# Beside the FFN: a unit's product on GpSimd, its split into planes on ScalarE, and one product of the ninth tile behind a unit

## Chip, cores and metric

The kernel runs on one core of one Trainium2 chip, as a single launch. The metric is the time of an execution on the device in microseconds. The profile names the engines PE (TensorE matmuls), PEld (TensorE weight loads), DVE (VectorE), ACT (ScalarE), POOL (GpSimd) and SP (SyncE, which here only issues DMAs).

## What is computed

Four sequences of 12544 positions and 128 channels go through a Hyena filter, a causal convolution as long as the sequence, and the result through a maxout FFN with three input matrices:

```
u = x * v                                        # (4, 12544, 128)
h = (relu(pos_emb @ w1) @ w2) * exp(-0.01*pos)   # (12544, 128)
y = irfft(rfft(u, 2S) * rfft(h, 2S))[:S]         # along the sequence
a = (x * y).reshape(4*12544, 128)
out = max(a @ W1, a @ W2, a @ W3) @ w_out        # d_ff = 768
```

## The kernel before

All arithmetic is in fp32. The Fourier transforms are products with constant matrices, in two stages: a first one over 98 blocks, a second one over the 128 positions of a block. The FFN's three-way maximum is rewritten: W1 is subtracted from W2 and W3, so a step makes `max(relu(a @ (W2-W1)), a @ (W3-W1))`, and W1's part is folded with `w_out` into one 128 x 128 matrix `lin` that is applied at the end of a tile.

**Order of the work.** The order is written out by hand; every engine runs its instructions in the order in which the program issues them. A prologue makes the filter's transform and the whole convolution of the first batch (to about 310 us). Then the FFN of batch b runs beside the convolution of batch b+1, for b = 0, 1, 2; the FFN of the last batch ends the kernel. A batch has 32 tiles of 4 x 98 = 392 columns, and a tile has six slots (one for each 128 rows of d_ff), so slot s = 6 i + f is step f of tile i. In a slot the loop calls `up` (two pairs of TensorE products into two of the three PSUM banks `hps`, a relu on ScalarE at L738, a maximum on VectorE at L741 that makes `hid`), then what is due of the down products, and then whatever the dictionaries `stream` and `beside` hold for this slot.

The first eight tiles (`TP = 8`) are taken in pairs with a Strassen-like scheme: their down products (L802) need sums of `hid` tiles that GpSimd makes (`sum_`, L771), and lie in `stream` several slots later, with banks `ops` and `cps3`; results leave through `copied` on ScalarE (L816) and `added` on VectorE (L819). From the ninth tile (i = 8) on, each tile is done by itself: `down` runs two slots late from the list `late`. At f = 0 it starts with the product of `lin` (L156, `ops<-gt,lin`) into the bank `ops`, which the last pair has used.

**Units.** `conv_steps` fills `beside`. The convolution's input for a batch is cut into 32 units of four channels each; in the first stage six units of batch 1 are made in the prologue, so 26, 32 and 32 units are made beside the three FFNs. A unit that is joined at slot s passes through:

- `u_load` (L354), slot s-9: SP issues the DMAs of `xr` and `vr` into two `ut` tiles of 128 x 392
- `u_mul` (L361), slot s-6: the product x * v in place, an elementwise product of two SBUF tiles
- `u_planes` (L381, L382), slot s-5: a memset of the padding and a copy that splits the fp32 numbers into two planes of uint16 halves, into one of three `planes` buffers (tag `cb`)
- `u_dma` (L388), slot s-4: SP issues a transposing DMA of the planes
- `u_join` (L397), slot s: two copies put the transposed halves together again, one on ScalarE and one on VectorE
- `unit` (L413 to L425), slot s+1: `u_first` twice, each 8 TensorE products (16 records in the trace) with the constant `f1q` into a bank `cps`, a copy `high` on ScalarE (L423), a sum and a difference `spec` on VectorE (L425)

The units follow each other every 1.5 to 1.6 slots and take the first 50 to 60 slots of a batch. After them come the pairs of frequencies (`g_quarter` and so on) in the remaining slots. In the same slots GpSimd also makes the sums and differences `t_sums` (L703) of the tile that comes two later, from the tiles `zt` that SP loads; `t_last` makes the tile's inverse transform and `gt`.

Of the kernel before, what the change touches and what calls it, by code (L numbers as in the profile page):

```python
# [13 lines left out]
ALU = mybir.AluOpType  # L14
# [77 lines left out]
def kernel(  # L92
# [15 lines left out]
    nc = tc.nc  # L108
# [247 lines left out]
            ts.append(t)  # L356
        us[u] = ts

    def u_mul(u):
        a, v = us[u]  # L360
        nc.vector.tensor_tensor(out=a[:], in0=a[:], in1=v[:], op=ALU.mult)  # L361

    def turn(u, ps):
        a, _ = us.pop(u)
# [13 lines left out]
    def u_planes(u):  # L378
        a, _ = us.pop(u)
        pl_ = cvp.tile([P, 2, 4, P], U16, tag="cb", name="planes", bufs=3)  # L380
        nc.gpsimd.memset(pl_[:, :, :, NB:], 0)  # L381
        nc.gpsimd.tensor_copy(  # L382
            pl_[:, :, :, 0:NB], a[:].bitcast(U16).rearrange("p s (n h) -> p h s n", h=2))
        us[u] = pl_

# [41 lines left out]
    def unit(u):  # L427
        for h in range(2):
            u_first(u, 2 * h, 2)
# [152 lines left out]
    def conv_steps(b, done):  # L582


        out = []

        def at(slot, late, fn, *args):
            out.append((slot, late, len(out), fn, args))

        for u in range(4, done):
            at(2 * u - 7, 1, unit, u)
        per_pair = 170 / (NK + LATE + 0.6 * (NU - done))
        for u in range(done, NU):
            s = (u - done) * 0.6 * per_pair + 9
            at(max(0, int(s) - 9), 0, u_load, b, u)
            at(int(s) - 6, 0, u_mul, u)
            at(int(s) - 5, 0, u_planes, u)
            at(int(s) - 4, 0, u_dma, u)  # L600
            at(int(s), 0, u_join, u)
            at(int(s + 1), 1, unit, u)
        s0 = int((NU - done - 1) * 0.6 * per_pair + 9) + 6

        def start(x):
            return s0 + int(x // 2 * 2 * per_pair)

        load = [0.6] * (NT * NF)
        for x in range(NK + LATE):
            s = start(x)  # L610
            load[s] -= 1.2
            load[s + 1 + x % 2] += 1.4

        def emptiest(among, cost):
            s = min(among, key=lambda i: load[i])
            load[s] += cost
            return s

        plan = []
        folds = {start(x) + 1 for x in range(NK + LATE)}  # L620
        for i in range(NT - 1):
            s = i * NF
            last = min((3, 4, 2), key=lambda k: s + k in folds)
            load[s + last] += 0.6
            if s <= s0:
                plan.append((0, 0, last))
                continue
            a = emptiest(range(s, s + 2), 0.7) - s
            plan.append((a, emptiest(range(s + a, s + max(a + 1, last - 1)), 0.7) - s, last))
        plan.append((3, 3, 4))  # L630

        for x in range(NK + LATE):
            s, odd = start(x), x % 2
            g, z = x if x < NK else None, x - LATE if x >= LATE else None
            at(s, 1, g_quarter, g, z)
            at(s + 1 + odd, 0, g_fold, g, z)
            at(max(s - 4, LOADS), 0, w_load, x)
            if z is not None:
                at(s + 3 + odd, 0, g_store, b, z)
            if g is None:  # L640
                continue
            if g % 2 == 0:
                at(max(s - 4, LOADS), 0, q_load, g, min(2, NK - g))
                at(s - 1, 0, h_load, g, min(2, NK - g))
            first = s + 2 + 2 * odd
            at(first, 0, q_swap, g, 0)
            at(first + 1, 0, q_swap, g, 64)
            last = start(x + LATE) - 1
            a = emptiest(range(first + 1, min(first + 3, last - 1) + 1), 0.7)
            at(a, 0, q_re, g)  # L650
            a = emptiest(range(a, min(first + 4, last - 1) + 1), 0.7)
            at(a, 0, q_im, g)
            two = sorted(emptiest(range(a + 1, last + 1), 0.55) for _ in range(2))
            for q in range(2):
                at(two[q], 0, q_unfold, g, q)
        slots = {}
        for s, _, _, fn, args in sorted(out, key=lambda r: r[:3]):
            slots.setdefault(s, []).append((fn, args))
        return slots, plan, s0
# [4 lines left out]
    TP = 8  # L664
# [187 lines left out]
    def run(steps):  # L852
        for fn, args in steps:
            fn(*args)
# [22 lines left out]
    def up_pair(b, i, h, j, tag=None):  # L877
        name, f = ORDER[j]
        own = ("hid", 3) if tag or name in sp["hid"] else (name, BUFS[name])
        h[name, f] = up((b, i + int(name[1]) - 1), f + (NC if name[2] == "2" else 0), *own)  # L880
# [46 lines left out]
    for i in range(9):  # L927
        if i < 8:
            mlp_in(i)
        if i:  # L930
            mlp_out(i - 1)
        if i in (4, 5):
            u_mul(i - 4)
        if i == 7:
            turn2(0)
# [3 lines left out]
    for f in range(0, FO, 4):  # L939
        quad([hs[:, f + i] for i in range(4)], (f1h[:, 0], f1h[:, 1]), specH[:, :, :, f:f + 4])  # L940
        u, k = divmod(f // 4, 4)
# [11 lines left out]
    for u in range(0, NU, 2):  # L953
        t = uts.pop(u)
        for v in range(2):
            if u + 4 < NU:
                u_mul(u + 4 + v)
            at = 4 * (u + v)
# [11 lines left out]
    for i in (1, 2):  # L970
        nc.vector.tensor_tensor(out=w_sb[i][:], in0=w_sb[i][:], in1=w_sb[0][:],
                                op=ALU.subtract)
# [173 lines left out]
    for n, (b, i) in enumerate(tiles[:LAST]):  # L1146
        if i == 0:
            beside, plan, pairs_from = conv_steps(b + 1, EARLY if b == 0 else 0)
            turns_.close()
            sp["pool"] = turns_.enter_context(tc.tile_pool(name="stp", bufs=1))  # L1150
            turn_of["of"] = 3
        if n == 0:
            t_load(*tiles[0])
            t_load(*tiles[1])
            t_sums(tiles[0], nc.vector)
            unit(2)
            t_last(tiles[0])
            unit(3)
            t_sums(tiles[1], nc.vector)
        for f in range(NF):  # L1160
            s = i * NF + f
            turn_ = i == NT - 1
            if i < TP:
                i0, j = i - i % 2, i % 2 * NF + f
                if j == 0:
                    h = {}
                    ends = i0 + 2 == TP
                if j in (0, 6 if ends else 4):
                    t_load(b, i0 + 2 + (j > 0))
                up_pair(b, i0, h, j)  # L1170
                if late:
                    down(*late.pop(0))
                if n == 0 and f == 0:
                    t_last(tiles[1])
                elif weights:
                    out, a1, a2 = weights.pop(0)
                    nc.vector.tensor_tensor(out=out, in0=a1, in1=a2, op=ALU.subtract)
                if j == 0:
                    banks = (obank, singles[3])
                    down_pair(b, i0, h, banks if i0 % 4 == 0 else banks[::-1], s, ends,  # L1180
                              1 if ends else 2)
            else:
                if i < NT - 2:
                    if f == 0:
                        t_load(*tiles[n + 2])
                elif turn_ and f < 2:
                    t_load(*tiles[n + 1 + f])
                if turn_ and f == 4:
                    t_sums(tiles[n + 2], nc.vector)
                h_ = up((b, i), f)  # L1190
            if i < TP and not ends:
                if j in (3, 7):
                    t_sums((b, i0 + 2 + (j > 3)))
            elif i >= TP - 1:
                for a in range(2):
                    if f == plan[i][a]:
                        t_sums(tiles[n + 1],
                               nc.vector if turn_ or i * NF > pairs_from else nc.gpsimd, (a,))
            run(stream.pop(s, ()))
            if i >= TP:  # L1200
                late.append(((b, i), f, h_))
                if len(late) > 2:
                    down(*late.pop(0))
            if i < TP and not ends:
                if j in (7, 10):
                    t_last((b, i0 + 2 + (j > 7)))
            elif i >= TP - 1:
                if f == plan[i][2]:
                    t_last(tiles[n + 1])
                if turn_ and f == 5:  # L1210
                    t_last(tiles[n + 2])
            if i >= TP and turn_of["of"] == 3 and not stream:
                turns_.close()
                wp = turns_.enter_context(tc.tile_pool(name="wp", bufs=3))
                hh = turns_.enter_context(tc.tile_pool(name="hh", bufs=2))
                turn_of["of"] = 4
            run(beside.pop(s, ()))
            if s == NT * NF - 1:
                assert not beside and not stream, sorted(beside)
# [72 lines left out]
```

## Time and profile before

| | us |
|---|---|
| median of 3 runs | 2301.78 |
| lowest, highest | 2295.15, 2305.05 |
| the profiled execution, its own time | 2307.12 |
| span of its profile | 2305.3 |

| group of the profile | count | busy us | mean ns |
|---|---|---|---|
| L361 on DVE, product of a unit (all 128 units) | 128 | 90.5 | 707 |
| L382 on POOL, copy into planes | 90 | 79.6 | 885 |
| L381 on POOL, memset of the padding | 90 | 26.6 | 295 |
| L397 on DVE, join | 90 | 87.7 | 975 |
| L397 on ACT, join | 90 | 70.1 | 779 |
| L771 on POOL, `s<-hid`, sums of the pairs | 84 | 94.7 | 1128 |
| L738 on ACT, relu | 768 | 382.5 | 498 |
| L741 on DVE, maximum | 768 | 427.8 | 557 |

Units are made beside the FFN from about 316 to 440 us, 834 to 984 us and 1357 to 1515 us of the span. A row of the timeline gives the start, the time taken, engine, line and operation, out<-in, the count of merged instructions, and in brackets how long the engine was idle before it and what ended that wait. "Busy" of PE is modelled, since matmuls overlap.

### The profile page before, as it was taken

The numbers are of one execution on the slowest core, as the hardware profiler recorded it, in microseconds if no ns is written. First come the engines' busy times: TensorE is split into PE (matmuls) and PEld (weight loads), VectorE is DVE, ScalarE is ACT, GpSimd is POOL, SyncE is SP. The second block draws the span as 40 slices with busy tenths as digits, with TensorE's granted clock in tenths as the row PEclk, the third lists the DMA queues.
The fourth block names the chain that finished last, engine by engine and source line by source line (L and its number), as shares of the span: only waits on it lengthen the run. The fifth ranks groups of instructions, "written<-read, shape, count | busy, mean of one in ns | idle before, by whom it ended". The sixth has DMA issues, their size and how long they took to land.

```text
span 2305.3 us, 70310 instructions
## 1 busy us (share of the span) xinstructions
PE 2260.9 (98%) x28383; PEld 1424.8 (62%) x28383; DVE 1605.3 (70%) x3102; ACT 1203.6 (52%) x2218; POOL 1015.8 (44%) x1207
## 2 busy tenths in 40 slices
PE   8999989999999999999999999999999999999998
PEld 7989857755555557755555557755555556666665
DVE  5588968757878768758887858757887854445443
ACT  2688845456666535546666635546666632222222
POOL 2044447613333347713333347723333326666666
PEclk9999989999999999999999999999999999999999
DMA  8779969789999669969999759969999832222221
GB/s 193 174 222 273 303 160 185 142 197 248 231 232 240 178 141 195 179 147 240 245 251 243 200 131 187 175 144 232 252 248 249 224 91 57 55 58 69 65 55 22
DMA packets 485568, 411.16 MB, mean 178 GB/s; under 512 B 341305, under 2 KB 387866, under 8 KB 485242
## 3 DMA queue, kind: packets, MB, share of 16 engines
q1 hardware_dynamic: 459778, 334.30, 64.9%
q0 software_dynamic: 24752, 70.65, 10.4%
q8 instruction: 223, 3.65, 0.7%
q10 hardware_dynamic: 712, 1.70, 0.3%
q14 instruction: 103, 0.84, 0.1%
HBM read 262.84 MB, written 84.67 MB: 151 GB/s over the span
## 4 chain that ended last, share of the span: by engine, by line
PE 78%; DMA 12%; DVE 3%; SPq 2%; POOL 2%; issue 1%; ACT 1%; POOLq 0%; DVEq 0%; ACTq 0%
PE hps L156 35%; PE ops L156 10%; PE ops L802 7%; PE cps L413 4%; DMA ht<-hd 4%; PE ps L156 3%; DMA wt<-wq_const 3%; PE cps L156 3%; PE ps L165 3%; DMA zt<-zd 2%; PE cps L472 2%; PE sps L1038 2%; PE cps L482 2%; PE cps L802 2%; PE gps L1020 2%; PE last L156 1%
## 5 line engine op out<-in xcount | busy, mean ns | idle before, releaser
L156 PE MATMUL hps<-gt,w_sb 128*64 128x392 f32 x6144 | 1149.2, 495 | 3.4 <-DVE hid L741 2.7
L738 ACT ACTIVATE hid<-hps 128x392 f32<-128x392 f32 x768 | 382.5, 498 | 720.5 <-PE hps L156 667.5
L156 PEld LDWEIGHTS hps<-gt,w_sb 128*64 128x64 f32 x6144 | 431.2, 137 | 418.5 <-issue 369.6
L741 DVE TENSOR_TENSOR hid<-hid,hps 128x392 f32<-128x392 f32 x768 | 427.8, 557 | 352.0 <-PE hps L156 342.9
L524 POOL TENSOR_TENSOR cb<-cb,xs 128x512 f32<-128x512 f32 x135 | 174.6, 1293 | 472.1 <-DVE xs L521 358.6
L156 PE MATMUL ops<-hid,wo_sb 128*64 128x392 f32 x1728 | 357.6, 492 | 0.0
L497 DVE TENSOR_TENSOR cb<-cps,eo 128x512 f32<-128x512 f32 (+1 forms) x288 | 175.1, 649 | 71.4 <-ACT eo L494 71.4
L156 PEld LDWEIGHTS ops<-hid,wo_sb 128*64 128x64 f32 x1728 | 124.2, 137 | 159.2 <-issue 159.0
L756 POOL DMA_DIRECT2D out_dram<-ot x72 | 56.6, 786 | 288.5 <-ACT ot L754 232.4
L512 ACT ACTIVATE xs<-cb 32x512 f32<-32x512 f32 x270 | 169.6, 628 | 19.7 <-DVE cb L497 10.9
L423 ACT COPY high<-cps 128x180 f32<-128x180 f32 x188 | 91.8, 490 | 147.6 <-PE cps L413 97.0
L513 ACT COPY xs<-cb 32x512 f32<-32x512 f32 x270 | 166.3, 616 | 3.2
L528 DVE TENSOR_TENSOR xs<-cb 128x256 f32<-128x256 f32 x270 | 147.7, 593 | 11.2 <-POOL cb L524 11.2
L413 PE MATMUL cps<-f1q,uT 98*64 98x90 f32 x3008 | 137.1, 242 | 5.8 <-DVE spec L425 3.0
L413 PEld LDWEIGHTS cps<-f1q,uT 98*64 98x64 f32 x3008 | 131.1, 138 | 14.2 <-issue 9.7
L425 DVE TENSOR_TENSOR spec<-cps,high 128x180 f32<-128x180 f32 x376 | 108.9, 338 | 42.5 <-ACT high L423 40.9
L771 POOL TENSOR_TENSOR s<-hid 128x392 f32<-128x392 f32 x84 | 94.7, 1128 | 78.2 <-DVE hid L741 52.0
L505 POOL DMA_DIRECT2D zd<-cb x135 | 92.9, 690 | 53.4 <-DVE cb L497 45.5
L361 DVE TENSOR_TENSOR ut<-ut 128x392 f32<-128x392 f32 x128 | 90.5, 707 | 32.2 <-DMA ut<-in_vr_dram 29.1
L771 POOL TENSOR_TENSOR s<-hid,s 128x392 f32<-128x392 f32 x84 | 91.6, 1091 | 42.2 <-DVE hid L741 41.9
L156 PEld LDWEIGHTS cps<-f4p,even 90*64 90x64 f32 x1568 | 90.0, 138 | 30.3 <-issue 27.6
L826 POOL DMA_DIRECT2D out_dram<-o x128 | 77.6, 611 | 51.3 <-DVE o L819 49.0
(147 smaller groups left out, 3592.1 us busy)
## 6 DMA issues: line engine op xcount, KB each, us to landing
ht<-hd SPq DMA_DIRECT2D x264, 256.0 KB, 7.0
wt<-wq_const SPq DMA_DIRECT2D x144, 256.0 KB, 7.0
zd<-cb POOLq DMA_DIRECT2D x135, 256.0 KB, 6.4
zt<-zd SPq DMA_DIRECT2D x384, 90.0 KB, 3.2
sq<-spec SPq DMA_DIRECT2D x264, 128.0 KB, 7.5
ut<-in_xr_dram SPq DMA_DIRECT2D x128, 196.0 KB, 4.1
ut<-in_vr_dram SPq DMA_DIRECT2D x128, 196.0 KB, 4.2
xT<-in_x_dram SPq DMA_DIRECT2D x256, 98.0 KB, 3.5
```

Source lines behind the costliest of these rows:

```text
L156: nc.tensor.matmul(out[64 * h:64 * h + 64], lhsT[:, 64 * h:64 * h + 64], rhs, start=start, stop=stop, skip_group_check=True)
L413: nc.tensor.matmul(ps[64 * c:64 * c + 64, 256 * i + h * N1:256 * i + (h + 1) * N1], t[:, 2 * ((at + i) % 8) + h].rearrange("n r t -> n (r ...
L425: nc.vector.tensor_tensor(out=spec[:, :, a, at:at + n], in0=v[:, 1], in1=high, op=op)
L497: nc.vector.tensor_tensor(out=cb[:, a, lo:hi], in0=ps[0][:, lo:hi], in1=eo[:, lo:hi], op=op)
L512: nc.scalar.mul(xs[at:at + 32], xt[at + 32:at + 64], -1.0)
L513: nc.scalar.copy(xs[at + 32:at + 64], xt[at:at + 32])
L524: nc.gpsimd.tensor_tensor(out=xts[g], in0=xts[g], in1=xs[:], op=ALU.add)
L528: nc.vector.tensor_tensor(out=ab[:, q], in0=y[:, 0], in1=y[:, 1], op=(ALU.subtract, ALU.add)[q])
L738: nc.scalar.activation(h[:], pa[:, 0:N], Relu)
L741: nc.vector.tensor_tensor(out=h[:], in0=h[:], in1=pb[:, 0:N], op=ALU.max)
L771: nc.gpsimd.tensor_tensor(out=out[:], in0=a[:], in1=b[:], op=op)
L802: nc.tensor.matmul(ps[64 * c:64 * c + 64, 0:H2], w, rhs[:, H2 * c:H2 * c + H2], start=start, stop=True, skip_group_check=True)
```

## The change

There are two edits. In `conv_steps` the product of a unit goes to GpSimd instead of VectorE (`u_mul` gets the engine as an argument; the products of the prologue stay on VectorE), and in `u_planes` the copy into the planes goes to ScalarE instead of GpSimd, while the memset stays on GpSimd. All slots stay as they are, so the GpSimd product comes one slot ahead of the ScalarE copy that reads it. The second edit concerns slot 50 (tile 8, f = 2): what `beside` holds for this slot, which is a unit's products, is issued ahead of the first `down` of tile 8, which is the product of `lin`, and no longer behind it.

```diff
-    def u_mul(u):
+    def u_mul(u, eng=nc.vector):
         a, v = us[u]
-        nc.vector.tensor_tensor(out=a[:], in0=a[:], in1=v[:], op=ALU.mult)
+        eng.tensor_tensor(out=a[:], in0=a[:], in1=v[:], op=ALU.mult)
...
         nc.gpsimd.memset(pl_[:, :, :, NB:], 0)
-        nc.gpsimd.tensor_copy(
+        nc.scalar.copy(
             pl_[:, :, :, 0:NB], a[:].bitcast(U16).rearrange("p s (n h) -> p h s n", h=2))
...
             at(max(0, int(s) - 9), 0, u_load, b, u)
-            at(int(s) - 6, 0, u_mul, u)
+            at(int(s) - 6, 0, u_mul, u, nc.gpsimd)
             at(int(s) - 5, 0, u_planes, u)
...
             run(stream.pop(s, ()))
+            if i == TP and f == 2:
+                run(beside.pop(s, ()))
             if i >= TP:
                 late.append(((b, i), f, h_))
                 if len(late) > 2:
                     down(*late.pop(0))
```

## The prediction

> **What bounds the kernel now.** Part 1 of the page came first. TensorE is busy nearly all the time; the others have room.
>
> ```profile
> PE 2260.9 (98%) x28383; PEld 1424.8 (62%) x28383; DVE 1605.3 (70%) x3102; ACT 1203.6 (52%) x2218; POOL 1015.8 (44%) x1207
> ```
>
> Next the stretches in which units of a batch are prepared beside the FFN of the batch before (busy us and counts of PE, PEld, DVE, ACT, POOL; then clock, DMA share, GB/s):
>
> ```profile
> 316.00:440.00 124.00, 121.89 (x1638) 90.31 (x1640) 100.32 (x216) 62.04 (x121) 90.83 (x107) 0.99 1.00 180
> 834.00:984.00 150.00, 146.93 (x1954) 107.62 (x1952) 116.14 (x252) 75.68 (x146) 115.30 (x131) 1.00 0.99 185
> 1357.00:1515.00 158.00, 151.56 (x1996) 110.33 (x1994) 115.93 (x255) 76.24 (x147) 115.13 (x131) 0.99 1.01 177
> ```
>
> Stretch less PE busy is 2.1, 3.1 and 6.4 us: 11.6 us of idle TensorE is about all that the change can win. VectorE is at 73 to 81%, GpSimd at 73 to 77%, ScalarE only at 48 to 50%. Where TensorE does wait is in its timeline:
>
> ```profile
> 331.10 1.54 PE L156 MATMUL hps<-gt,w_sb 128*64 128x392 f32 x8 [0.50 <-DVE hid L741]
> ...
> 851.08 1.54 PE L156 MATMUL hps<-gt,w_sb 128*64 128x392 f32 x8 [1.11 <-DVE hid L741]
> 853.69 0.55 PE L802 MATMUL cps<-s,tw 128*64 128x196 f32 x4 [0.73 <-POOL s L771]
> 978.25 0.88 PE L156 MATMUL ops<-gt,lin 128*64 128x392 f32 x4 [0.45 <-DVE o L819]
> 1475.83 1.47 PE L413 MATMUL cps<-f1q,uT 98*64 98x90 f32 x16 [2.76 <-DVE spec L425]
> ```
>
> The pair at 851 and 853 recurs at 1374 and 1377, the 0.45 us at 460 and 1506. Last, GpSimd's timeline at the start of the second batch: no gaps, so GpSimd runs behind the order of the program there.
>
> ```profile
> 841.42 1.49 POOL L703 TENSOR_TENSOR zt<-zt 90x512 f32<-90x512 f32 x1
> 842.87 1.35 POOL L771 TENSOR_TENSOR s<-hid,s 128x392 f32<-128x392 f32 x1
> 844.16 0.30 POOL L381 MEMSET planes<- 128x240 uint16 x1
> 844.40 0.84 POOL L382 COPY planes<-ut 128x784 uint16<-128x784 uint16 x1
> ```
>
> The relus of ScalarE are at the pace of TensorE at the same time:
>
> ```profile
> 842.08 0.50 ACT L738 ACTIVATE hid<-hps 128x392 f32<-128x392 f32 x1 [0.82 <-PE hps L156]
> 843.40 0.50 ACT L738 ACTIVATE hid<-hps 128x392 f32<-128x392 f32 x1 [0.82 <-PE hps L156]
> ```
>
> **What the Trainium skill says.** "SBUF — State Buffer", Who interferes with whom: a VectorE instruction with two SBUF inputs contends with a GpSimd instruction that reads SBUF, and the second waits for the first; ScalarE waits for nobody. The trace agrees: the product L361 takes 534 ns at its shortest and up to 2987 ns beside GpSimd. "ScalarE: Activation LUTs", What ACT_TABLE_LOAD costs: an ACTIVATE with immediates is 186 ns + 0.833 ns an element. No run here shows that copy on ScalarE.
>
> **The change, part by part.** 90 units are prepared this way (26, 32, 32).
>
> *Removed from VectorE:* 90 products L361. In these stretches one takes about 0.73 us (19.02 us for 26), so some 65 us of VectorE, and its waits for the `ut` DMA (1.1 + 4.1 + 8.7 us in the three stretches). Nothing of that was on TensorE's path except where a hid maximum (L741) or a spec sum (L425) stood behind a product: the 0.50 us at 331 (gone), the 1.11 us at 851 and 1374, and the 2.76 us at 1475, where VectorE had sat until 1474.61 for `ut`.
>
> *GpSimd:* takes 90 products; the same shape there is L771 at 1059 to 1128 ns, I take 1.06 us. It loses 90 copies L382 at 0.885 us. Net 90 x 0.175 = +16 us, or about +5 us in each stretch of 25 to 43 us of GpSimd idle. The memset L381 stays on GpSimd, one slot behind the product. Queued behind a product that waits for its `ut` DMA are the t_sums and the Strassen sums L771; TensorE needs the latter some slots later.
>
> *ScalarE:* 90 copies of 784 uint16 elements. The nearest row is L397 on ScalarE, 512 strided uint16 elements in 779 ns; 272 more at the page's 0.833 ns give 1.0 us. Bounds 0.84 us (the page's formula alone) and 1.2 us (779 x 784/512). That is +90 us on an engine that has 62 to 82 us idle in each stretch, so the work itself I cost at nothing: the cover is ScalarE's 0.8 to 1.75 us gap ahead of most relus and `high` copies; without it each copy would delay a relu by its 1.0 us.
>
> *The new wait:* each copy waits on ScalarE, in order, for the GpSimd product issued one slot earlier; relu and `high` stand behind it, and behind them L741, L425 and TensorE's PSUM banks (three hps banks in turn: a relu must end before the second product of the next slot). At 842: GpSimd ends zt at 842.9 and the product at 844.0, the copy ends at 845.0, so the relu due at 842.08 is 2.9 us late; the bank is wanted 0.8 us after the relu would have ended: TensorE loses 2.1 us. The second copy: sum, memset, product (1.05 + 0.3 + 1.06) end at 846.4, another 1.1 us. The third is hidden; ahead of the fourth GpSimd has two sums L703 of 1.28 us and one L771, and 1.5 us go. Together 4.7 us, less the 1.11 + 0.73 us lost there already, less some 0.4 us since sums of 1.35 us fall back towards 1.05 us without L361 on the shared port: +2.5 us. The third batch has the same pattern: +2.5 us. Bounds: 0 us if GpSimd catches up earlier, 5 us if nothing of the present losses is saved. The first batch starts with GpSimd waiting for hid, not behind: 0.4 us against 0.50 us gained, 0.
>
> *Steady state:* placing the new instructions between their neighbours in the trace, GpSimd would end the product more than 1 us after ScalarE wants it for 20 of the other 78 units, 35 us in sum. There a slot lasts 2 to 3.3 us instead of 1.3, so a relu 1 to 2 us late still meets its bank. I take +1 us; bounds -3 and +18 us (half the lateness).
>
> *SP:* the issues of `ut`, zt and the transposes keep their order. A transpose now waits for ScalarE's copy, up to 2 us later than GpSimd's was; the join comes four slots later (some 10 us) and landing takes 4.4 us, so I cost it at nothing. If that cover is gone, `ut` and zt behind it land later and GpSimd's products wait.
>
> *1475:* the `ut` DMA lands as late as before (GpSimd product about 1475.7), so ScalarE waits in VectorE's place, but one slot later: half of 2.76, -1.4 us (bounds -2.8 and 0).
>
> *Folded product:* the unit's 16 + 16 records L413 go ahead of `ops<-gt,lin`, which waited for VectorE's `o`. They fill 3 x 0.45 = -1.4 us (bounds -2 and 0).
>
> Sum: 5.0 + 0 + 1.0 - 1.4 - 1.4 = **+3 us** on the profiled execution's 2307.1 us. The median of the runs shown, 2301.8 us, is 5.3 us lower; +3 us on it is 2305, and as the steady state may give back a little by VectorE's free time I say **2304 us**.
>
> **Rivals.** (1) *Faster:* VectorE was the hidden limit. Then the start-ups cost nothing and most of the 11.6 us goes: -8 to -11 us, 2292. For it: VectorE at 73 to 81% and waits that name it. Against: TensorE waits in few places. (2) *Slower:* ScalarE held in order by GpSimd in the steady state, priced above: 18 us of lateness reach TensorE on top of the start-ups, 2301.8 + 5 + 18 = 2325; the milder half is 2314. It decides from where GpSimd's lateness plus 1.0 us exceeds ScalarE's gap of about 1.5 us plus about 1.3 us of bank slack. For it: GpSimd at 75% with long runs without a gap, and the transposes that feed back through SP. Against: ScalarE at 50%. (3) *It doesn't do what it says:* VectorE's free time isn't used since TensorE is at its own rate; that is the forecast without start-up losses, 2300.
>
> **Numbers.** Forecast with (3): 0.66. Rival (2): 0.24. Rival (1): 0.10. A measurement of this kernel can tell about 0.5% (11.5 us) from no change. The range 2293 to 2319 takes in the bounds of the start-ups and of 1475, and most of rival (2)'s milder half. Faster by over 0.5%: 0.09; within: 0.67; slower: 0.24.
>
> **What would show it.** Right: ScalarE waits for GpSimd's `ut` product before L382 near 842 and 1366, TensorE's idle time there larger by 2 to 3 us a batch; no DVE `o` ahead of the lin product; L382 on ScalarE near 1.0 us; GpSimd's L361 near 1.1 us. Wrong: waits of L738 or L423 behind L382 throughout, with TensorE's idle in the stretches above 20 us (rival 2), or below 5 us (rival 1).

## The result and the profile after

The change makes the kernel slower by 14 us: 2315.80 us (median of 6 runs, 2309.42 to 2322.61) against 2301.61 us (6 runs, 2295.15 to 2310.25). The ratio is 1.0058, with a 95% interval of 1.0031 to 1.0086. That is inside the range given and 12 us above the value; a slowdown of more than 0.5% had been given a chance of 0.24.

The profiled execution took 2315.6 us with a span of 2313.8 us, so the two traces differ by 8.5 us and not by 14: the profiled execution of before is 5 us above its own median. What follows explains these 8.5 us; of the rest no trace tells.

The engines of the kernel after, part 1 of its page:

```profile
PE 2262.3 (98%) x28383; PEld 1434.3 (62%) x28383; DVE 1556.6 (67%) x3012; ACT 1259.6 (54%) x2308; POOL 1017.9 (44%) x1207
```

VectorE has 90 instructions fewer, ScalarE 90 more, and GpSimd kept its count (90 went and 90 came): the change does what it says. VectorE is busy 49 us less, and the kernel is slower all the same. The stretches in which units are prepared (busy us and counts of PE, PEld, DVE, ACT, POOL, then clock, DMA share and GB/s):

```profile
316.00:440.00 124.00, 122.00 (x1655) 90.35 (x1653) 86.40 (x192) 80.16 (x148) 93.28 (x108) 1.00 0.95 179
834.00:985.00 151.00, 141.44 (x1864) 105.73 (x1862) 94.36 (x211) 90.73 (x172) 110.58 (x129) 0.98 0.96 174
1357.00:1515.00 158.00, 150.34 (x2008) 110.25 (x2006) 101.01 (x223) 93.58 (x177) 113.13 (x131) 0.99 0.94 176
```

TensorE is idle for 2.0, 9.6 and 7.7 us, 19.2 us in place of 11.6 (the second stretch is 1 us longer than the one shown of before). Its clock in the second stretch fell to 0.98.

**Where the time went.** With the TensorE products of `hps` of both traces numbered from the first, the difference of their start times (after less before) at some points, and what each stretch between them added:

| before's time, us | after less before, us | added | what lies in the stretch |
|---|---|---|---|
| 842 | -2.5 | -2.5 | first batch; the `lin` product at 463 is 0.7 of it, a half clock that ended sooner 1.7 (see below) |
| 877 | -1.4 | +1.1 | start of the second batch |
| 896 | +2.3 | +3.7 | a place near 890 |
| 932 | +1.6 | -0.7 | |
| 968 | +7.9 | +6.3 | a place near 957 |
| 1356 | +5.1 | -2.8 | `lin` at 979: -0.7; -2.1 at 1038 and 1153, away from the change |
| 1383 | +6.7 | +1.5 | start of the third batch |
| 1419 | +11.6 | +4.9 | a place near 1416 |
| 1456 | +10.0 | -1.6 | |
| 1477 | +6.2 | -3.8 | the wait at 1475 that before had |
| 1519 | +6.2 | 0.0 | +0.7, then `lin` at 1507: -0.7 |
| 2290 | +8.4 | +2.2 | at 1650 to 1685, where no unit is prepared |

Three places, near 890, 957 and 1416, cost 14.9 us together. All other rows together give back 6.5 us. The losses and gains at 1038, 1153 and 1660 lie outside the stretches of the change and sum to nothing; their cause is open.

**What happens at the three places.** Groups of the kernel after:

```profile
L397 DVE COPY uT<-turned 98x512 uint16<-98x512 uint16 x90 | 94.6, 1051 | 0.0
L361 POOL TENSOR_TENSOR ut<-ut 128x392 f32<-128x392 f32 x90 | 93.4, 1037 | 76.5 <-DMA ut<-in_vr_dram 67.9 <-DVE uT L397 3.7 <-DVE hid L741 2.5
L382 ACT COPY planes<-ut 128x784 uint16<-128x784 uint16 x90 | 76.2, 847 | 46.9 <-POOL ut L361 40.1 <-DMA turned<-planes 6.5
```

The moved instructions cost what was estimated or less: the copy L382 0.85 us (1.0 forecast), the product 1.04 us (1.06). The row that matters is the first: VectorE's half of the join, which the change does not touch, rose from 975 ns to 1051 ns on average. The line view of before and then of after gives the shortest, median and longest in ns:

```profile
L397 DVE COPY uT<-turned x90: 446/837/3107, 336.8 to 1527.1; 98x512 uint16<-98x512 uint16 x90
```

```profile
L397 DVE COPY uT<-turned x90: 439/918/5082, 337.1 to 1533.3; 98x512 uint16<-98x512 uint16 x90
```

The same copy takes 0.44 us or 5.08 us. The waits of TensorE, summed over the kernel (us, times, longest), first before and then after, name the same tile:

```profile
PE cps L413 <- DVE uT L397: 2.3, 5, 0.9
...
PE ops L156 <- DVE o L819: 1.4, 3, 0.5
```

```profile
PE cps L413 <- DVE uT L397: 10.3, 5, 3.6
PE hps L156 <- ACT hid L738: 6.7, 7, 1.6
```

8.5 of the 10.3 us are three waits (1.76, 3.60 and 3.12 us), one at each of the three places. The first of them in the timelines of VectorE, GpSimd and TensorE of the kernel after (start, us, engine, operation, wait before it):

```profile
887.62 4.12 DVE L397 COPY uT<-turned 98x512 uint16<-98x512 uint16 x1
891.64 0.54 DVE L741 TENSOR_TENSOR hid<-hid,hps 128x392 f32<-128x392 f32 x1
```

```profile
887.97 1.03 POOL L771 TENSOR_TENSOR hid<-hid 128x392 f32<-128x392 f32 x1
888.94 0.31 POOL L381 MEMSET planes<- 128x240 uint16 x1
889.19 1.03 POOL L361 TENSOR_TENSOR ut<-ut 128x392 f32<-128x392 f32 x1
890.17 1.01 POOL L771 TENSOR_TENSOR hid<-hid 128x392 f32<-128x392 f32 x1
891.12 0.30 POOL L381 MEMSET planes<- 128x240 uint16 x1
891.38 1.21 POOL L771 TENSOR_TENSOR hid<-hid 128x392 f32<-128x392 f32 x1
```

```profile
891.88 1.53 PE L413 MATMUL cps<-f1q,uT 98*64 98x90 f32 x32 [1.76 <-DVE uT L397]
893.14 2.88 PE L156 MATMUL hps<-gt,w_sb 128*64 128x392 f32 x8
```

The copy starts at 887.62 and ends only at 891.7, while GpSimd goes from sum to product to sum without a gap. TensorE waits 1.76 us for it. Then eight products of `hps` take 2.88 us where they mostly take 1.54: the granted clock was 0.50 for 3.41 us from 893.1. A window of after at the second place and two windows of the low clock show both halves of the loss:

```profile
955.60:958.90 3.30, 0.65 (x8) 0.29 (x4) 3.30 (x1) 1.38 (x2) 3.30 (x5) 1.00 1.15 173
961.40:964.80 3.40, 3.40 (x17) 2.19 (x15) 1.65 (x5) 1.70 (x3) 0.48 (x2) 0.50 1.12 120
1425.70:1429.00 3.30, 3.30 (x16) 1.77 (x14) 1.68 (x5) 1.72 (x4) 0.00 (x0) 0.50 1.00 215
```

In the first, VectorE spends the whole 3.3 us in one instruction, GpSimd is busy throughout, and TensorE works for 0.65 us. In the others TensorE is fully busy, at half the clock. So a place costs the wait and then, by estimate, 1.7 us, half of a 3.41 us stretch: 8.5 + 3 x 1.7 = 13.6 us. The second place has one more wait, of 1.04 us at 951, which is not of this kind (see the steady state below).

"SBUF — State Buffer", Who interferes with whom, states that a VectorE copy in a two-port mode takes a port pair that it shares with GpSimd, and that the second to come is held for the whole of the first one's instruction. The trace does not name the mode of this copy. It agrees on the direction and goes further: the five GpSimd instructions shown up to the memset at 891.12 all ended while the copy at 887.62 was held, not one alone.

### The profile page after: what moved, and what is told of

It is laid out like the page before. It is cut to its first block, busy times and chain, and to the rows that moved or that the text cites. A ratio compares the mean times of both kernels' runs of the same rounds, so it can differ in the third digit from the quotient of the medians.

```text
span 2313.8 us, 70422 instructions
## 1 busy us (share of the span) xinstructions
PE 2262.3 (98%) x28383; PEld 1434.3 (62%) x28383; DVE 1556.6 (67%) x3012; ACT 1259.6 (54%) x2308; POOL 1017.9 (44%) x1207
## 3 DMA queue, kind: packets, MB, share of 16 engines
q0 software_dynamic: 24752, 70.65, 10.3%
## 4 chain that ended last, share of the span: by engine, by line
PE 82%; DMA 9%; DVE 3%; POOL 2%; issue 2%; SPq 1%; ACT 1%; POOLq 0%; DVEq 0%; ACTq 0%
PE hps L156 37%; PE ops L156 11%; PE ops L802 7%; PE cps L413 4%; PE ps L156 3%; PE cps L156 3%; PE ps L165 3%; DMA ht<-hd 3%; PE cps L472 2%; DMA sq<-spec 2%; PE cps L482 2%; PE cps L802 2%; PE sps L1038 2%; PE gps L1020 2%; PE last L156 1%
## 5 line engine op out<-in xcount | busy, mean ns | idle before, releaser
L413 PE MATMUL cps<-f1q,uT 98*64 98x90 f32 x3008 | 137.4, 243 | 11.7 <-DVE uT L397 10.3
L413 PEld LDWEIGHTS cps<-f1q,uT 98*64 98x64 f32 x3008 | 132.5, 138 | 16.6 <-issue 14.5
L423 ACT COPY high<-cps 128x180 f32<-128x180 f32 x188 | 87.1, 495 | 91.2 <-PE cps L413 59.2
L361 POOL TENSOR_TENSOR ut<-ut 128x392 f32<-128x392 f32 x90 | 93.4, 1037 | 76.5 <-DMA ut<-in_vr_dram 67.9
L771 POOL TENSOR_TENSOR s<-hid 128x392 f32<-128x392 f32 x84 | 87.6, 1043 | 78.7 <-DVE hid L741 52.7
L771 POOL TENSOR_TENSOR s<-hid,s 128x392 f32<-128x392 f32 x84 | 86.8, 1034 | 38.5 <-DVE hid L741 38.2
L382 ACT COPY planes<-ut 128x784 uint16<-128x784 uint16 x90 | 76.2, 847 | 46.9 <-POOL ut L361 40.1
```

The source lines that it names most:

```text
L413: nc.tensor.matmul(ps[64 * c:64 * c + 64, 256 * i + h * N1:256 * i + (h + 1) * N1], t[:, 2 * ((at + i) % 8) + h].rearrange("n r t -> n (r ...
L771: nc.gpsimd.tensor_tensor(out=out[:], in0=a[:], in1=b[:], op=op)
```

## The experiments

Two theories were tested. "Before" is the kernel before, run again beside each series. **A**: VectorE's join copy is locked out by GpSimd's runs without a gap, and TensorE then idles and loses half of its clock for a while. **B**: ScalarE, held in order behind GpSimd's product, is the cost.

**The second edit alone**, on the kernel before.

```diff
             run(stream.pop(s, ()))
+            if i == TP and f == 2:
+                run(beside.pop(s, ()))
```

> The kernel before with the second edit alone (the unit's products ahead of the lin product of the ninth tile). Both theories: the three TensorE waits of 0.45 us for VectorE's o go and nothing else moves; 1.4 to 2 us less than before in the profile, ratio 0.999 to 1.000.

Measured: 2300.08 us against 2301.05, ratio 0.9991 [0.998, 1.0002]. The three waits of the `lin` product for VectorE's `o` are gone. The edit is good for about a microsecond at most, which this number does not tell from nothing, and it is not what made the kernel slower.

**The product alone on GpSimd**; the copy into planes stays on GpSimd too.

```diff
-        nc.vector.tensor_tensor(out=a[:], in0=a[:], in1=v[:], op=ALU.mult)
+        eng.tensor_tensor(out=a[:], in0=a[:], in1=v[:], op=ALU.mult)
...
-            at(int(s) - 6, 0, u_mul, u)
+            at(int(s) - 6, 0, u_mul, u, nc.gpsimd)
```

> The kernel before with the product on GpSimd alone; the split into planes stays on GpSimd, so ScalarE waits for nothing new. Theory A (VectorE's join copies, L397, are locked out by longer runs of GpSimd without a gap; TensorE then sits idle and loses its clock): GpSimd now has product and split, its runs are longer still, L397 copies of 4 us and more are at least as many as in the kernel after (3), TensorE's clock drops at least three times, time 8 to 30 us above before. Theory B (ScalarE, held in order by GpSimd's product, is the cost): that wait is gone, time within 3 us of before.

Measured: 2322.49 us, ratio 1.0075 [1.0047, 1.0102]. Its line view has the join copy at up to 6.5 us, but its largest losses have another cause, in the timeline of TensorE:

```profile
L397 DVE COPY uT<-turned x90: 441/885/6476, 335.0 to 1542.0; 98x512 uint16<-98x512 uint16 x90
```

```profile
855.52 0.92 PE L802 MATMUL cps<-s,tw 128*64 128x196 f32 x4 [4.72 <-POOL s L771]
```

GpSimd with both jobs is busy 131 of the 151 us from 834 to 985, and the sums of the pairs come late. Here the clock fell for 10.24 us at once. One part of A's expectation failed: of join copies of 4 us and more, at least three were expected and one came (the next took 3.99 us). So the number fits A, yet only part of it is A's mechanism; GpSimd's plain lateness is a third cause, which the full change avoids since the planes leave GpSimd. B's expectation, within 3 us of before, fails too, but because of that third cause this run alone cannot decide between the two.

**The planes alone on ScalarE**, the product staying on VectorE.

```diff
-        nc.gpsimd.tensor_copy(
+        nc.scalar.copy(
             pl_[:, :, :, 0:NB], a[:].bitcast(U16).rearrange("p s (n h) -> p h s n", h=2))
```

> The kernel before with the split into planes on ScalarE alone; the product stays on VectorE. Theory A: GpSimd reads SBUF for 80 us less, no L397 on VectorE above 3.2 us, no clock drop that before does not have; time equal to before or up to 6 us less. Theory B: ScalarE waits in order for VectorE's product, which itself waits for its load (29 us of waits in before), so relus come late: 2 to 8 us above before.

Measured: 2300.36 us, ratio 0.9993 [0.9984, 1.0003]; the longest join copy is 2.72 us. ScalarE's 90 copies, and its waiting in order for another engine's product, cost nothing that shows. A's expectation came, B's did not.

**The join off the shared port.** The whole change, with VectorE's half of the join written as a reduction over an axis of length one: same engine, same place in its order, same data. Later expectations call it the one-port join.

```diff
+    def reduced(out, in_):
+        nc.vector.tensor_reduce(out=out, in_=in_.rearrange('n s r (t o) -> n s r t o', o=1), op=ALU.max, axis=mybir.AxisListType.X)
+
+    one_port = (nc.scalar.copy, reduced)
...
-            copies[h](
+            one_port[h](
```

> The kernel after with VectorE's half of the join made as a maximum over an axis of length one (tensor_reduce[...]) in place of a copy. Theory A: L397 on VectorE takes about 0.6 to 0.8 us each time, never 2 us; the three waits of TensorE of 1.8 to 3.6 us and the clock drops behind them go; some 12 to 15 us less than after in the profile, ratio to before 0.997 to 1.001; the start-ups at 842 and 1366 still lose 1.4 us each. Theory B: nothing of this changes the time, ratio 1.004 to 1.008.

Measured: 2297.36 us, ratio 0.9981 [0.9971, 0.999], 18 us less than the change by medians and by spans (2295.8 against 2313.8), where 12 to 15 us were expected. The line view of this kernel, where the reduction is recorded at L153 and later lines are five higher:

```profile
L153 DVE TENSOR_REDUCE uT<-turned x90: 718/734/766, 334.3 to 1517.5; 98x512 uint16<-98x512 uint16 x90
```

90 joins within 48 ns of each other. "SBUF — State Buffer", Who interferes with whom, states that such a reduction never contends on this chip; this run agrees. From 313.8 to 2293.6 us the clock never falls, and TensorE's wait for the join is 0.2 us in all:

```profile
PE hps L161 <- ACT hid L743: 7.0, 8, 1.6
...
PE cps L418 <- DVE uT L153: 0.2, 1, 0.2
```

ScalarE still waits 39.4 us for GpSimd's product in this kernel (40.1 us in the change), and GpSimd 65.7 us for the `ut` DMA (67.9 us). Both waits stay and the time goes: neither was what cost these 18 us. This settles A against B. What it does not show is that missing gaps of GpSimd are what holds the copy.

**Both halves of the join on ScalarE**, with the whole change: the lockout removed in a second way.

```diff
-            copies[h](
+            nc.scalar.copy(
```

> The kernel after with both halves of the join copied on ScalarE[...]. Theory A (lockout of VectorE's copy): the waits of TensorE near 890, 956 and 1420 and the clock drops go, as with the one-port form; ScalarE takes 90 more copies of 0.78 us and may give some back; 2298 to 2308 us. Theory B (ScalarE held in order is the cost): ScalarE is more loaded and waits longer, 2314 to 2325 us.

Measured: 2301.16 us, ratio 0.9995 [0.9985, 1.0006], span 2300.2 us, and no low clock from 315.2 to 2295.0 us. The three places are gone as well. By its median it is less good than the reduction, though the intervals overlap. ScalarE now has 90 more copies, and TensorE's waits for `uT` are replaced by 3.6 us of waits before L413 that ScalarE's relu ended (1.9 us with the reduction).

**The reduction alone on the kernel before.**

```diff
-            copies[h](
+            one_port[h](
```

> The kernel before with the one-port join alone (the maximum over an axis of length one), neither edit of the change. It tells what the change is worth once VectorE's join cannot be locked out. Theory A: before lost little to lockouts (its longest copy was 3.1 us, one clock drop at 1475), so 0 to 4 us less than before, 2297 to 2301, no better than the kernel after with the one-port join within 4 us either way. Theory B: after with the one-port join would be slower than this by 5 us or more.

Measured: 2303.62 us, ratio 1.0001 [0.9989, 1.0013]. The gain of up to 4 us that was expected did not come. The join copies of before, up to 3.1 us, cost TensorE 2.3 us, and the waits moved to others: its waits for VectorE's `spec` sums before the unit's products are 5.7 us here, 3.0 us in before, and two of them, of 1.97 and 2.10 us, were followed by a clock of 0.50. So in the kernel before, the held copies cost nothing that shows, and the port freed does not by itself make a faster kernel. The run also tells what the change is worth once the copy cannot be held: 0.9981 with it against 1.0001 without, by estimate 4.6 us faster. The two series ran apart and their intervals just touch, so the size is rough.

**The start-ups.** To the kernel with the reduction, the sums L703 of the first tiles that come next go to VectorE while the first pair of tiles is worked on (`i0` is the pair's first tile).

```diff
-                    t_sums((b, i0 + 2 + (j > 3)))
+                    t_sums((b, i0 + 2 + (j > 3)), nc.gpsimd if i0 else nc.vector)
```

> The kernel after with the one-port join, and the sums L703 of the first two tiles that come up in a batch on VectorE in place of GpSimd: GpSimd's backlog at the start of a batch is then 5 us shorter when ScalarE asks for its first products. If the start-up losses are ScalarE's wait for a late GpSimd product: ScalarE's waits before the first four split copies (2.4, 0.9, 0.6, 2.7 us) and TensorE's waits for relus near 840 to 849 and 1363 to 1372 (1.6, 0.6, 0.9 us) shrink by more than half, 2 to 4 us less than with the one-port join alone. If they come from elsewhere: they stay, time the same or 1 to 2 us more.

Measured: 2295.85 us, ratio 0.9975 [0.9967, 0.9983]; span 2293.8 us. ScalarE's waits for GpSimd before the first four copies at 837 to 846 are 0, 0.94, 0 and 0 us, and the relu waits of TensorE's `hps` products, 7.0 us with the reduction alone, fall to 0.2:

```profile
PE hps L161 <- DVE hid L746: 5.2, 3, 1.9
...
PE hps L161 <- ACT hid L743: 0.2, 1, 0.2
```

Part of it came back as waits for VectorE's maximum (5.2 us, 1.8 with the reduction alone), which now stands behind those sums. The waits show that the start-up losses were ScalarE's wait for a late product. The gain in time, 2 us by the traces, is at the low end of the 2 to 4 us expected, and the intervals of the two kernels overlap. The median is the lowest of all kernels here, about 6 us below before.

**The same without the product's move**: before with the planes on ScalarE, the second edit and the reduction; the product stays on VectorE.

> A version meant to be faster: product on VectorE as in before, split on ScalarE, the ninth tile's product behind the unit, and the one-port join. VectorE has one instruction with two SBUF inputs per unit left, GpSimd 80 us less to do. Expected 4 to 8 us less than before, 2293 to 2297 us, and 0 to 4 us less than after with the one-port join; if ScalarE's wait for VectorE's product matters, it is equal to or slower than that.

Measured: 2297.48 us, ratio 0.9977 [0.9967, 0.9987]. Within the intervals this equals the kernel with the product on GpSimd (0.9981). With the join copy out of the way no difference shows between the two engines for the product.

## Why the prediction was right or wrong

**The start-ups: right in mechanism, half in size.** ScalarE waits for GpSimd's product there, in the timeline of ScalarE after:

```profile
841.17 0.85 ACT L382 COPY planes<-ut 128x784 uint16<-128x784 uint16 x1 [2.43 <-POOL ut L361]
843.35 0.85 ACT L382 COPY planes<-ut 128x784 uint16<-128x784 uint16 x1 [0.94 <-POOL ut L361]
845.56 0.85 ACT L382 COPY planes<-ut 128x784 uint16<-128x784 uint16 x1 [0.57 <-POOL ut L361]
850.32 0.85 ACT L382 COPY planes<-ut 128x784 uint16<-128x784 uint16 x1 [2.66 <-POOL ut L361]
```

TensorE, in its timeline, loses time at three of the four:

```profile
842.46 1.54 PE L156 MATMUL hps<-gt,w_sb 128*64 128x392 f32 x8 [1.63 <-ACT hid L738]
844.65 0.88 PE L156 MATMUL hps<-gt,w_sb 128*64 128x392 f32 x4 [0.65 <-ACT hid L738]
...
851.62 0.87 PE L156 MATMUL hps<-gt,w_sb 128*64 128x392 f32 x3 [0.87 <-ACT hid L738]
```

2.1, 1.1, 0 and 1.5 us were forecast; 1.63, 0.65, 0 and 0.87 us came, to a few hundredths the same in the third batch. The net is +1.1 and +1.5 us by the table, for +2.5 each. The first copy ended at 842.02, which is 844.5 in the time of before (its start-up lies 2.5 us later), where 845.0 was worked out: 0.35 us because GpSimd's product was that much earlier, 0.15 us because the copy takes 0.85 us and not 1.0. The lower bound given for it (0.84 us, from "ScalarE: Activation LUTs") was close (0.85 us measured); building on the strided row L397 was not.

**The steady state: the step that failed.** "I take +1 us; bounds -3 and +18 us" was worked out from how late ScalarE would be. That part was about right. Apart from the start-ups, TensorE's `hps` products wait for a relu for 0.4 us in the whole kernel (6.7 us less two start-ups of 3.15), and 1.04 us more was lost at one place, in the timelines of ScalarE and TensorE after:

```profile
949.45 0.85 ACT L382 COPY planes<-ut 128x784 uint16<-128x784 uint16 x1 [2.54 <-POOL ut L361]
950.20 0.78 ACT L423 COPY high<-cps 128x180 f32<-128x180 f32 x2
```

```profile
951.44 0.84 PE L413 MATMUL cps<-f1q,uT 98*64 98x90 f32 x16 [1.04 <-ACT hid L738]
```

ScalarE waited for GpSimd's product, so its copies `high`, which read the `cps` banks, came late; the trace puts TensorE's wait down to the relu that stands behind them. But some 13.9 us of the three places also lie in this term, and they come from VectorE. The prediction used the shared port for L361 and the sums, and counted the port as freed once L361 had left VectorE. It did not ask which other VectorE instructions take it. The join copy does. The sign was in the trace of before: L397 on VectorE had a mean of 975 ns where its shortest took 446.

Why the same copy fared better before stays open. It is tempting to say that GpSimd lost its gaps: before, its copy L382 waited for VectorE's product, 13.5, 14.8 and 16.1 us in the three stretches. But it waits for the `ut` DMA instead, and from 316 to 440, 834 to 985 and 1357 to 1515 us it is idle for 116.0 us in all after and for 111.7 us before. So it has no fewer gaps; they lie elsewhere. What the traces do show is that the long holds go with the product on GpSimd: the change has three joins of 4.12 to 5.08 us and the product alone has two of 3.99 and 6.48 us, while before, the second edit alone and the planes alone have none above 3.13 us. By what rule the held copy is let in between two GpSimd instructions no run here shows.

**VectorE's 65 us: rightly costed at nothing.** With the reduction, the kernel with the product left on VectorE is as fast as the one with it on GpSimd (0.9977 and 0.9981).

**GpSimd's +16 us: costed at nothing, right for the count.** The sums L771 became shorter (1043 ns from 1128 for `s<-hid`), so GpSimd's busy time rose by 2 us only. (GpSimd's least idle time in a stretch, given as 25 us, is 33 us by the lines shown: 124 less 90.83.) What was wrong is the thought that only the amount counts: what GpSimd's instructions did to VectorE's copy counted for more.

**SP at nothing: right as far as the time shows.** GpSimd waits 67.9 us for `ut` in the change, where VectorE waited 29.1 us in before, but it waits about as long (65.7 us) in the faster kernel with the reduction.

**1475 and the folded product: right sign, too small.** -1.4 us was said for 1475 and -3.8 came. The wait there was 2.76 us and the clock was 0.50 for 3.41 us after it, which the prediction had not seen in the trace of before; without the wait both go. The three `lin` products gained 0.70 us each, not 0.45. The first batch gained 1.8 us beside its `lin` product, where nothing was forecast; 1.7 us of it is the half clock at its start, which lasts to 321.6 us in the trace of before and to 316.3 us in that of after. The change touches nothing there, and in the ten traces it ends anywhere from 311.5 to 321.6 us: that gain is luck.

**The rivals.** The slower one gives 2314 to 2325 us, and 2315.8 came, but not by its mechanism: waits behind ScalarE in the steady state come to 1.4 us only. The rivals left out a slow case in which VectorE is the one that is held. The range reached 2319 because it was to take in part of that rival, so it is luck that the number lies within it. The sum of +3 us was off in the other direction as well: with the join as a reduction the change makes the kernel about 4 us faster (0.9981).

## What to carry to other kernels

When work is moved to GpSimd, list every VectorE instruction that remains beside it and may use the shared port, copies within SBUF among them, and compare the shortest with the longest duration of each in the trace: a wide spread of one shape is the warning. Busy time alone does not price such a move: GpSimd's rose by 2 us, its idle time in the stretches did not fall, and 14 us were lost all the same. A wait of TensorE is to be priced with the half clock that may follow it.

## What the runs showed of the hardware

- Beside GpSimd, a VectorE copy of 98x512 uint16 took from 0.44 us, when free, to 6.48 us. The same data through a reduction over an axis of one took 718 to 766 ns in all of 90 times: slower than the free copy, yet faster than the mean of the copies in the change, 1051 ns.
- After TensorE waits of 1.76, 3.60 and 3.12 us the granted clock was 0.50 for 3.41 us. "TensorE: Matmul & The Clock Gate", Part 1: The HAM clock gate, tells of half a clock after an idle window of about 3.4 us, on a window that runs free. The length agrees, but less than a whole window was enough here.
- The traces tell how much less. In each of the ten, the stretches of low clock start whole multiples of 3.41 us apart, so they lie on a grid. Cut along it, the ten traces have 5742 windows from 322 to 2285 us. TensorE was idle (by its modelled busy time) for 1.76 us or more in 15 of them, about half a window, and 14 of these were followed by a window at 0.50; the exception had 1.87 us, at 838.5 in the kernel with its first sums on VectorE. No window with less was followed by one, save two that were at 0.50 themselves, in the kernel with the product alone on GpSimd. So what counts is the idle time within a window, not the length of one wait: of the 3.60 us wait, 1.75 us fell in a window after which the clock stayed, and 1.85 us in the next, after which it fell. In the kernel with the planes alone on ScalarE, waits of 0.71 and 1.07 us in one window were enough.
